# Attention with top-k and a gated FFN on one core: sums over V in units of the last 64 queries over a full 128-row last chunk of keys

## The chip, the cores and the metric

The kernel runs on one core of a Trainium2 chip. The metric is the device time of one execution in microseconds; the time before is the median of three runs. The core's engines work side by side and meet at semaphores: PE (TensorE, matmuls and transposes), DVE (VectorE), ACT (ScalarE), POOL (GpSimd) and SP, which here only issues DMA transfers.

## What is computed

Eight batches, eight heads, 576 queries and keys a head, head dimension 64; everything is fp32. A head's scores are masked to the 32 largest of each query, run through a softmax and multiplied with V. The result is the input of a gated FFN.

```python
def _attn_ref(q, k, v):                      # each (8, 8, 576, 64)
    scores = scale * np.matmul(q, k.transpose(0, 1, 3, 2))
    kth = np.partition(scores, -top_k, axis=-1)[..., -top_k:-top_k + 1]
    scores = np.where(scores >= kth, scores, -1000000000.0)
    scores = scores - np.max(scores, axis=-1, keepdims=True)
    attn = np.exp(scores)
    attn = attn / (np.sum(attn, axis=-1, keepdims=True) + 1e-09)
    return np.matmul(attn, v).astype(np.float32)

def _moe_ref(x, w_gate, w_val, w_out):       # x (4608, 512), d_ff 1536
    g = x @ w_gate
    silu = g * (1.0 / (1.0 + np.exp(-g)))
    return (silu * (x @ w_val) @ w_out).astype(np.float32)
```

## The kernel before

The 576 queries of a head are four groups of 128 and one of 64 (`P` = 128, `J` = 4, `R` = 64, `S` = 576, `JP` = 512). The keys are cut in the same way: four chunks of 128 and a tail of 64. A unit of work is one query group of one pair of heads: `units` lists for each batch the groups `qt` = 0 to 4 and for each group the four pairs of heads, 160 units in all. In an ordinary unit the two heads lie side by side in the free dimension, 2 x 576 scores for each of 128 queries. In a unit of the last 64 queries (`qt == J`, called `last` in the code; 32 units) the two heads are stacked on the partitions: 64 queries of one head on partitions 0 to 63, 64 of the other on 64 to 127, with one row of 576 scores each.

The main loop runs over the units, one step each, with the stages of several units in one step. `scores` (L314, L300 for last units) multiplies Q and K on PE, ACT scales the result into `sc` (L319, L305); `select` finds the 32 largest on DVE (L334, L338); `weigh` runs the exponentials on ACT (L361, L366); `normalize` divides by the sum, on ACT (L384) or POOL (L386). Two steps after a unit's selection `turn` transposes its weights `e` on PE (L400), so that keys come onto the partitions: four chunks of 128 columns into one PSUM bank, then the tail; ACT copies them to `et` (L401). In a last unit the tail is 64 columns, and its transposed form has 64 rows.

`values` (L434), for two units at a time, multiplies V and `et`, with V as the stationary operand. A head's sum is accumulated over its five chunks of keys; the two heads of a pair write to partitions 0 to 63 and 64 to 127 of `av`, and their matmuls alternate. In an ordinary unit the 64-key tail is joined over two heads: `vlast` is a 128x128 block of which the off-diagonal quarters are zero. In a last unit the tail is summed with `v_last`, 64 rows of V for each of the two heads, after the four full chunks: eight matmuls with 128 rows and 64 columns of V and 64 moving columns, then two with 64 rows. ACT copies `av` to `xT` (L450), the input of the FFN.

Blocks of FFN matmuls (`feed`, L578 and L644) are spread between these stages by credits. The order of instructions on PE, DVE, ACT and POOL is the order in which the program writes them, tied at the end of the kernel (L912 on). Within a step PE gets: the scores of a later unit, `values` of two earlier units (in every second step), the scores of one more unit, then pieces of the FFN, the transposes and the pieces that remain.

V of a pair of heads is loaded by `load_v` on SP's queue: the 512 full keys (L243), the tail for last units (L247) and the tail for ordinary units (L250, two transfers). The loads for the next batch are issued right after `values` has read the buffers of this batch for the last time; `slabs` has four buffers for `v` and for `v_last`. POOL's first work is the identity; its next is the rounding of the FFN weights (L121, L122).

Of the kernel before, what the change touches and what calls it, by code (L numbers as in the profile page):

```python
# [10 lines left out]
FP32 = mybir.dt.float32  # L11
# [4 lines left out]
P = 128  # L16
# [9 lines left out]
def kernel(  # L26
# [37 lines left out]
    nc = tc.nc  # L64
    B, H, S, D = q.shape
    DM, DFF = w_gate.shape
    J = S // P
    JP = J * P
    R = S - JP
# [10 lines left out]
    consts = ctx.enter_context(tc.tile_pool(name="consts", bufs=1))  # L80
    ld = ctx.enter_context(tc.tile_pool(name="ld", bufs=2))
    slabs = ctx.enter_context(tc.tile_pool(name="slabs", bufs=4))
# [7 lines left out]
    ident = consts.tile([P, P], FP32, name="ident")  # L90
    make_identity(nc, ident[:])
    NV = 4
    vlast = []
    for i in range(NV):
        vt = consts.tile([P, P], FP32, name=f"vlast{i}")
        nc.vector.memset(vt[:], 0.0)
        vlast.append(vt)
    wg = consts.tile([P, KC, DFF], FP32, name="wg")
    wv = consts.tile([P, KC, DFF], FP32, name="wv")
    wo = consts.tile([P, MC, DM], FP32, name="wo")  # L100
# [136 lines left out]
    def load_v(i):  # L237
        b, hp = pairs[i]
        h = slice(2 * hp, 2 * hp + 2)
        vt = slabs.tile([P, 2, J, D], FP32, tag="v", name="v")  # L240
        v_last = slabs.tile([R, 2, D], FP32, tag="vl", name="v_last")
        vl = vlast[i % NV]
        nc.sync.dma_start(  # L243
            vt[:].rearrange("p h j d -> p h (j d)"),
            v[b, h, 0:JP].rearrange("h (p j) d -> p h (j d)", j=J),
        )
        nc.sync.dma_start(v_last[:], v[b, h, JP:S].rearrange("h p d -> p h d"))  # L247
        for hh in range(2):
            o = hh * R
            nc.sync.dma_start(vl[o : o + R, o : o + R], v[b, 2 * hp + hh, JP:S])  # L250
        vs[i] = (vt, v_last, vl)
# [138 lines left out]
    def turn(n):  # L390

        last = units[n][1] == J
        e = state[n].pop("e")
        et = work.tile([P, 2 * J + 1, P], FP32, tag="et", name="et")
        for c0, cn in ((0, J), (J, 1)) if last else ((0, J), (J, 1), (J + 1, J)):
            ps = ps_t.tile([P, 512], FP32, tag="t", name="etps")
            kl = R if last and c0 == J else P
            for c in range(cn):
                k0 = (c0 + c) * P
                nc.tensor.transpose(ps[0:kl, c * P : (c + 1) * P], e[:, k0 : k0 + kl], ident[:])  # L400
            nc.scalar.copy(  # L401
                et[0:kl, c0 : c0 + cn, :],
                ps[0:kl, 0 : cn * P].rearrange("p (c j) -> p c j", c=cn),
            )
            if c0 == J:
                yield
        state[n]["et"] = et
# [3 lines left out]
    def values(ns):  # L411

        b, qt, hp0 = units[ns[0]]
        last = qt == J
        ql = R if last else P
        av = ps_t.tile([P, 2, P], FP32, tag="t", name="av")
        for i, n in enumerate(ns):
            assert units[n] == (b, qt, hp0 + i)
            vt, v_last, vl = vs[b * NHP + hp0 + i]
            et = state.pop(n)["et"]  # L420
            for c in (*range(J), J) if last else (J, *range(J)):
                kl = R if last and c == J else P
                for hh in range(2):
                    d = slice(hh * R, (hh + 1) * R)
                    if c == J:
                        weights_, at = (v_last[:, hh, :], d) if last else (vl[:, d], None)
                    else:
                        weights_, at = vt[:, hh, c, :], d if last else None
                    moving = (
                        et[0:kl, c, at]  # L430
                        if last
                        else et[:, c + (0 if c == J else hh * (J + 1)), :]
                    )
                    nc.tensor.matmul(  # L434
                        av[d, i, 0:ql],
                        weights_,
                        moving,
                        start=c == (0 if last else J),
                        stop=c == (J if last else J - 1),
                    )  # L440
        c0 = b * S + qt * P
        at = c0
        hps = slice(hp0, hp0 + len(ns))
        while at < c0 + ql:
            kb = at // BLK
            n_c = min((kb + 1) * BLK, c0 + ql) - at
            if kb not in xT:
                xT[kb] = ffn.tile([P, NHP, BLK], FP32, tag="xT", name="xT", bufs=3)
                done[kb] = 0
            nc.scalar.copy(  # L450
                xT[kb][:, hps, at - kb * BLK : at - kb * BLK + n_c],
                av[:, 0 : len(ns), at - c0 : at - c0 + n_c],
            )
            done[kb] += n_c * len(ns)
            at += n_c
# [364 lines left out]
    def finish_units(ns):  # L820
        values(ns)
        for n in ns:
            b, qt, hp = units[n]
            if qt == J and b + 1 < B:
                load_v((b + 1) * NHP + hp)
# [17 lines left out]
    for n in range(NU + 3):  # L843
# [41 lines left out]
        if n < NHP:  # L885
            load_v(n)
# [4 lines left out]
        if 0 <= n - TURN < NU:  # L891
            run(turn(n - TURN))
# [63 lines left out]
```

## Time and profile before

| | |
|---|---|
| runs | 1759.61, 1762.16, 1762.41 us; median 1762.16 |
| profiled execution | 1759.77 us, of which the span from the first to the last instruction is 1758.0 |
| mean granted TensorE clock | 0.974 of full speed |
| tail transposes and others, L400 | 1312 matmul records, 182.9 us busy |
| sums over V, L434 | 2560 records with `v`, 512 with `vlast`, 128 with `v_last` |
| copies of `et`, L401 | 448, 183.4 us busy |
| loads of `v_last` | 32 of 32 KB, 3.1 us from issue to landing |

A record of a matmul says its form as rows x columns of the stationary operand (128*64: 128 rows of contraction, 64 columns) and then the moving operand. Matmuls are pipelined, and the profile models their ends; their starts are taken from the hardware, so the distance from one start to the next tells what each costs a busy PE. The granted clock is the share of full speed that PE had; it is recorded in stretches that are multiples of 3.4 us, at 1.0 or at 0.5.

### The profile page before, as it was taken

How to read it: one execution, taken by the hardware profiler on the slowest of the kernel's cores; microseconds unless marked ns; L12 is line 12 of the kernel's file. 1: busy time of each engine (PE TensorE's matmuls, PEld its weight loads, DVE VectorE, ACT ScalarE, POOL GpSimd, SP SyncE). 2: the span in 40 equal slices, each digit the busy share in tenths (PEclk: the TensorE clock that was granted, in tenths of full speed). 3: DMA queues.
4: the chain of work that ended last, by engine and by line, in shares of the span. 5: the costliest groups of instructions: out<-in, count | busy, mean ns of one | idle time of the engine just before them, and what ended most of it. 6: DMA issues, size and time to landing. Idle time of an engine off the chain costs nothing.

```text
span 1758.0 us, 31754 instructions
## 1 busy us (share of the span) xinstructions
PE 1679.6 (96%) x11408; PEld 1404.5 (80%) x11408; DVE 1476.5 (84%) x3311; ACT 1262.3 (72%) x2901; POOL 798.8 (45%) x910
## 2 busy tenths in 40 slices
PE   5578999999999999999999999999999999999999
PEld 3468588787888788887888878887888878788887
DVE  6999899989889899898899898898988988898300
ACT  7899787777767686768776777777776777676431
POOL 4898534343353425352535334443444433535434
PEclk6698999999999999999999999999999999999999
DMA  7442120003000120002100020000300020000000
GB/s 200 138 120 86 29 68 1 13 2 83 15 13 1 28 70 1 13 12 59 28 13 1 14 70 27 1 13 19 78 2 13 1 57 15 13 1 13 1 13 12
DMA packets 109309, 59.72 MB, mean 34 GB/s; under 512 B 88544, under 2 KB 96992, under 8 KB 109152
## 3 DMA queue, kind: packets, MB, share of 16 engines
q1 hardware_dynamic: 108016, 57.37, 12.5%
q8 instruction: 90, 1.47, 0.4%
q14 instruction: 67, 0.55, 0.1%
q10 hardware_dynamic: 1136, 0.33, 0.1%
HBM read 48.23 MB, written 9.44 MB: 33 GB/s over the span
## 4 chain that ended last, share of the span: by engine, by line
PE 81%; DVE 8%; ACT 8%; POOL 1%; issue 1%; DMA 1%; SPq 0%; ACTq 0%; POOLq 0%
PE f L578 37%; PE av L434 9%; PE x_ps L644 9%; PE s L314 7%; PE y_ps L644 7%; PE etps L400 6%; DVE m L334 4%; DVE e L338 3%; PE f L494 3%; ACT e L366 2%; PE s L300 2%; PE kqps L267 1%; ACT e L361 1%; ACT et L401 1%; PE o_ps L546 1%
## 5 line engine op out<-in xcount | busy, mean ns | idle before, releaser
L334 DVE MAX8 m<-e 128x8 f32<-128x576 f32 x864 | 615.0, 748 | 3.1
L338 DVE MATCH_REPLACE8 e<-m,e 128x576 f32<-128x576 f32 x576 | 423.9, 743 | 0.0
L578 PE MATMUL f<-xT,wg 128*128 128x256 f32 x1536 | 355.0, 381 | 0.0
L578 PE MATMUL f<-xT,wv 128*128 128x256 f32 x1536 | 353.9, 380 | 0.0
L578 PEld LDWEIGHTS f<-xT,wg 128*128 128x128 f32 x1536 | 287.7, 190 | 45.7 <-issue 8.4
L578 PEld LDWEIGHTS f<-xT,wv 128*128 128x128 f32 x1536 | 286.8, 190 | 42.7 <-issue 5.5
L614 POOL TENSOR_TENSOR h<-h,half_g 128x512 f32<-128x512 f32 x96 | 122.5, 1276 | 352.7 <-ACT h L613 336.8
L366 ACT ACTIVATE e<-e,bias 128x576 f32<-128x576 f32 x288 | 221.2, 776 | 34.1 <-POOL bias L349 30.9
L400 PE MATMUL etps<-ident,e 128*128 128x128 f32 (+1 forms) x1312 | 182.9, 281 | 46.7 <-POOL e L386 19.3
L400 PEld LDWEIGHTS etps<-ident,e 128*128 128x128 f32 (+1 forms) x1312 | 154.3, 143 | 76.9 <-POOL e L386 25.3
L338 DVE MATCH_REPLACE8 e<-m,sc 128x576 f32<-128x576 f32 x288 | 211.9, 742 | 0.0
L361 ACT ACTIVATE e<-sc,m 128x576 f32<-128x576 f32 x288 | 211.3, 786 | 0.0
L334 DVE MAX8 m<-sc 128x8 f32<-128x576 f32 x288 | 203.3, 743 | 7.5 <-ACT sc L319 7.5
L319 ACT ACTIVATE sc<-s 128x288 f32<-128x288 f32 x512 | 167.5, 414 | 53.4 <-PE s L314 53.0
L619 POOL TENSOR_TENSOR h<-h,val 128x512 f32<-128x512 f32 x96 | 122.5, 1276 | 178.5 <-ACT val L618 166.0
L386 POOL TENSOR_TENSOR e<-e,tot 128x576 f32<-128x576 f32 x140 | 160.8, 1152 | 87.4 <-DVE tot L380 76.2
L401 ACT COPY et<-etps 128x512 f32<-128x512 f32 (+1 forms) x448 | 183.4, 489 | 12.2 <-PE etps L400 11.7
L314 PE MATMUL s<-kqT 64*128 64x288 f32 x1024 | 171.3, 444 | 16.4 <-ACT et L401 8.3
L379 DVE TENSOR_SCALAR tot<-tot 128x1 f32<-128x1 f32 x228 | 29.4, 146 | 172.0 <-ACT e L366 171.9
L434 PE MATMUL av<-et,v 128*64 128x128 f32 (+1 forms) x2560 | 158.7, 267 | 0.0
L384 ACT ACTIVATE e<-e,tot 128x576 f32<-128x576 f32 x148 | 118.5, 801 | 46.5 <-DVE tot L380 46.2
L314 PEld LDWEIGHTS s<-kqT 64*128 64x128 f32 x1024 | 95.1, 191 | 62.2 <-issue 24.0
(85 smaller groups left out, 2279.0 us busy)
## 6 DMA issues: line engine op xcount, KB each, us to landing
v<-in_v_dram SPq DMA_DIRECT2D x32, 256.0 KB, 3.4
kq_in<-in_k_dram SPq DMA_DIRECT2D x63, 128.0 KB, 2.9
kq_in<-in_q_dram SPq DMA_DIRECT2D x63, 128.0 KB, 3.3
w<-in_moe_w_gate_dram SPq DMA_DIRECT2D x12, 512.0 KB, 3.9
w<-in_moe_w_val_dram SPq DMA_DIRECT2D x12, 512.0 KB, 3.7
w<-in_moe_w_out_dram SPq DMA_DIRECT2D x12, 512.0 KB, 3.6
out_dram<-o SPq DMA_DIRECT2D x38, 128.0 KB, 2.4
out_dram<-o SPq DMA_DIRECT2D x16, 256.0 KB, 2.4
```

The lines of the kernel that those rows point to most:

```text
L314: nc.tensor.matmul(ps[:, 0:half], slab[d, q0 : q0 + P], slab[d, k0 : k0 + half])
L319: nc.scalar.mul(sc[:, i * half : (i + 1) * half], ps[:, 0:half], scale)
L334: nc.vector.max(m[:, t, 8 * r : 8 * r + 8], cur[:, hs])
L338: nc.vector.match_replace(e[:, hs], m[:, t, 8 * r : 8 * r + 8], cur[:, hs], LOWEST)
L361: nc.scalar.activation(e[:, hs], sc[:, hs], AF.Prelu, bias=m[:, t, TOP_K - 1 : TOP_K], scale=-1.0, alpha=SMALL,)
L366: nc.scalar.activation(e[:, hs], e[:, hs], AF.Exp, bias=bias[:, t : t + 1], scale=-1.0 / SMALL, accum_out=tot[:, t : t + 1],)
L386: nc.gpsimd.tensor_tensor(e[:, hs], e[:, hs], tot[:, t : t + 1].to_broadcast([P, S]), ALU.mult)
L400: nc.tensor.transpose(ps[0:kl, c * P : (c + 1) * P], e[:, k0 : k0 + kl], ident[:])
L401: nc.scalar.copy(et[0:kl, c0 : c0 + cn, :], ps[0:kl, 0 : cn * P].rearrange("p (c j) -> p c j", c=cn),)
L434: nc.tensor.matmul(av[d, i, 0:ql], weights_, moving, start=c == (0 if last else J), stop=c == (J if last else J - 1),)
L578: nc.tensor.matmul(ps[:, i, :], w[:, kc, m * P : (m + 1) * P], x[:, kc, :], start=(kc == 0), stop=(kc == KC - 1),)
L644: nc.tensor.matmul(ps, lhsT, T[i][m], start=m == 0, stop=m == MQ - 1)
```

## The change

The tail of a last unit becomes the last 128 keys (448 to 575) in place of the last 64 (512 to 575). Its transpose takes 128 columns of `e`, the copy to `et` 128 partitions, and the two matmuls 128 rows. The keys 448 to 511 thus come in twice, once with the fourth chunk and once here; the second time they meet rows of zeros. V's tail now lies on partitions 64 to 127 of `vtail`, and partitions 0 to 63 are zeroed once, at the start, by four memsets on POOL. The four `vtail` tiles are fixed buffers, taken in turn by the pair's number; the pool's tag `vl` with its four buffers goes. Ordinary units are as they were.

```diff
@@ -90,11 +90,14 @@
     ident = consts.tile([P, P], FP32, name="ident")
     make_identity(nc, ident[:])
     NV = 4
-    vlast = []
+    vlast, vtail = [], []
     for i in range(NV):
         vt = consts.tile([P, P], FP32, name=f"vlast{i}")
         nc.vector.memset(vt[:], 0.0)
         vlast.append(vt)
+        vt = consts.tile([P, 2, D], FP32, name=f"vtail{i}")
+        nc.gpsimd.memset(vt[0 : P - R], 0.0)
+        vtail.append(vt)
     wg = consts.tile([P, KC, DFF], FP32, name="wg")
     wv = consts.tile([P, KC, DFF], FP32, name="wv")
     wo = consts.tile([P, MC, DM], FP32, name="wo")
@@ -238,13 +241,13 @@
         b, hp = pairs[i]
         h = slice(2 * hp, 2 * hp + 2)
         vt = slabs.tile([P, 2, J, D], FP32, tag="v", name="v")
-        v_last = slabs.tile([R, 2, D], FP32, tag="vl", name="v_last")
+        v_last = vtail[i % NV]
         vl = vlast[i % NV]
         nc.sync.dma_start(
             vt[:].rearrange("p h j d -> p h (j d)"),
             v[b, h, 0:JP].rearrange("h (p j) d -> p h (j d)", j=J),
         )
-        nc.sync.dma_start(v_last[:], v[b, h, JP:S].rearrange("h p d -> p h d"))
+        nc.sync.dma_start(v_last[P - R : P], v[b, h, JP:S].rearrange("h p d -> p h d"))
         for hh in range(2):
             o = hh * R
             nc.sync.dma_start(vl[o : o + R, o : o + R], v[b, 2 * hp + hh, JP:S])
@@ -394,13 +397,12 @@
         et = work.tile([P, 2 * J + 1, P], FP32, tag="et", name="et")
         for c0, cn in ((0, J), (J, 1)) if last else ((0, J), (J, 1), (J + 1, J)):
             ps = ps_t.tile([P, 512], FP32, tag="t", name="etps")
-            kl = R if last and c0 == J else P
             for c in range(cn):
-                k0 = (c0 + c) * P
-                nc.tensor.transpose(ps[0:kl, c * P : (c + 1) * P], e[:, k0 : k0 + kl], ident[:])
+                k0 = S - P if last and c0 == J else (c0 + c) * P
+                nc.tensor.transpose(ps[:, c * P : (c + 1) * P], e[:, k0 : k0 + P], ident[:])
             nc.scalar.copy(
-                et[0:kl, c0 : c0 + cn, :],
-                ps[0:kl, 0 : cn * P].rearrange("p (c j) -> p c j", c=cn),
+                et[:, c0 : c0 + cn, :],
+                ps[:, 0 : cn * P].rearrange("p (c j) -> p c j", c=cn),
             )
             if c0 == J:
                 yield
@@ -419,7 +421,6 @@
             vt, v_last, vl = vs[b * NHP + hp0 + i]
             et = state.pop(n)["et"]
             for c in (*range(J), J) if last else (J, *range(J)):
-                kl = R if last and c == J else P
                 for hh in range(2):
                     d = slice(hh * R, (hh + 1) * R)
                     if c == J:
@@ -427,7 +428,7 @@
                     else:
                         weights_, at = vt[:, hh, c, :], d if last else None
                     moving = (
-                        et[0:kl, c, at]
+                        et[:, c, at]
                         if last
                         else et[:, c + (0 if c == J else hh * (J + 1)), :]
                     )
```

## The prediction

> **What bounds the kernel now.** I read the page's busy shares first, then its chain of waits, then busy times by stretch, and last the matmuls around the sums over V in order of time.
>
> ```profile
> PE 1679.6 (96%) x11408; PEld 1404.5 (80%) x11408; DVE 1476.5 (84%) x3311; ACT 1262.3 (72%) x2901; POOL 798.8 (45%) x910
> ...
> PE 81%; DVE 8%; ACT 8%; POOL 1%; issue 1%; DMA 1%; SPq 0%; ACTq 0%; POOLq 0%
> ```
>
> PE is busy 96% of the span and makes 81% of the chain that ended last. A busy PE isn't PE at its peak, so the stretches come next (columns: length, then busy time of PE, weight loads, DVE, ACT, POOL, granted clock, DMA share).
>
> ```profile
> 345.00:600.00 255.00, 252.88 (x1725) 211.79 (x1725) 228.19 (x519) 186.09 (x426) 110.89 (x133) 1.00 0.08 20
> 600.00:900.00 300.00, 297.21 (x2036) 249.57 (x2036) 268.19 (x614) 223.82 (x523) 120.41 (x145) 1.00 0.13 33
> 900.00:1200.00 300.00, 298.78 (x1993) 251.37 (x1992) 269.01 (x615) 221.04 (x508) 127.07 (x150) 1.00 0.07 19
> 1200.00:1500.00 300.00, 296.79 (x2039) 248.19 (x2038) 266.00 (x607) 222.02 (x517) 122.21 (x148) 1.00 0.11 27
> ```
>
> From 345 us on PE stands still for about 1% of the time, at full clock, and DVE has some 11% to spare. What is taken from PE there should come off the end. Now the sums over V. A matmul of fp32 leaves two records (64 matmuls with `v_last` on 64x64 give 128), which I call passes. First a block of a pair of units with the last 64 queries, then one of ordinary units:
>
> ```profile
> 226.64 0.69 PE L434 MATMUL av<-et,v 128*64 128x64 f32 x16
> 227.25 0.33 PE L434 MATMUL av<-et,v_last 64*64 64x64 f32 x4
> 227.52 0.69 PE L434 MATMUL av<-et,v 128*64 128x64 f32 x16
> 228.13 0.33 PE L434 MATMUL av<-et,v_last 64*64 64x64 f32 x4
> 228.39 1.00 PE L314 MATMUL s<-kqT 64*128 64x288 f32 x6
> ...
> 269.63 0.44 PE L434 MATMUL av<-et,vlast 128*64 128x128 f32 x4
> 269.90 1.04 PE L434 MATMUL av<-et,v 128*64 128x128 f32 x16
> 270.77 0.39 PE L434 MATMUL av<-et,vlast 128*64 128x128 f32 x4
> 270.99 1.04 PE L434 MATMUL av<-et,v 128*64 128x128 f32 x16
> ```
>
> No idle is noted in the first block, yet the rate differs. Sixteen passes of form 128*64 go from 226.64 to 227.25, 38 ns each; the four of form 64*64 take 227.25 to 227.52, 68 ns each. In the ordinary block, all of one form, four passes of twice as many columns cost 0.22 us (270.77 to 270.99), 55 ns each. So the tail is dear although it streams least. The starts of single matmuls show where the time lies. Between passes of one form with 64 columns the steps alternate, 7 ns and 52 ns (a pair of heads every 58.5 ns). From the last `v` pass to the first `v_last` pass the step is 152 ns (median of 28 after 340 us), from the last `v_last` pass to the next unit's `v` 148, to the scores that follow 148, and inside the four tail passes 7, 100, 7. A change of tile at the same form costs no such step: `vlast` to `v`, both 128*64 with 128 columns, is 103 ns (104 times), the usual step there, while `v` to the scores' 64*128 is 203. A change of form thus costs about 100 ns, whichever way I compare (152 less 52, 203 less 103).
>
> **The change, part by part.** *Tail matmuls (L434).* They keep their number and order; the form goes from 64*64 to 128*64, that of the `v` passes. For the first unit of a block, last `v` pass to the next unit's first `v` pass is now 152 + 113 + 148 = 413 ns. In one form it is three pair pitches less one short step, 3 x 58.5 - 7 = 169 ns, so 244 ns go. For the second unit the change of form ahead of the scores stays: 413 becomes 52 + 65 + 149 = 266, so 147 go. Together 0.39 us for a block. There are 32 units of this kind in 16 blocks. Fifteen run at full clock: 15 x 0.39 = 5.9 us. The last, at 1690.4 to 1693.3 us, runs at half clock (steps 244, 168, 242, pair pitch 108): 654 becomes 324 - 7 = 317, and 654 becomes about 101 + 115 + 242 = 458, which saves 0.53 us. Sum 6.4 us. Bounds: by changes of form alone, three fewer a block at 100 ns, 16 x 0.3 = 4.8 us; by the whole surplus 6.4. I take 6.4, since the restart inside the tail (100 for 52) follows a change of form each time and nowhere else.
>
> The Trainium skill, "TensorEngine Tiling (Array Packing)", Key Properties, says that changing the tiling mode, not just the tile, drains TensorE; the rows above agree, with 100 ns as the price. A rule of the same page, Theoretical Speedup, speaks against the change: with 64 rows of contraction two row tiles can work at once, up to twice as fast, and 128 rows give that up. If the tail used that today, its two pairs at 58.5 ns would be half price and the change would give back 32 x 58.5 = 1.9 us; by that the sum would be 4.5 us. Here both heads' tails lie on partitions 0 to 63, hence in one row tile, and start 7 ns apart exactly as the 128*64 passes do, so I take nothing off.
>
> *Tail transposes (L400).* Each of 32 takes 128 columns of `e` as weights for 64. Where they run unheld, the step to and from the narrow one is 109 ns, the same as between full ones; no form cost shows. Cost 0; bounds 0 and, if the weight load (108 ns at the least, 140 in the median) were exposed, 32 x 0.03 = 1.0 us.
>
> *Tail copies (L401).* ACT copies 128x128 in place of 64x128. Single copies of 64 partitions took 265 ns in the median (32), of 128 partitions 286 (125). The nearest bounds are 0 and 32 x 0.02 = 0.7 us of ACT. ACT is busy 72%; the copy is made one to two steps ahead of its reader, which hides it. Without that cover it costs the 0.7. I take 0.
>
> *Four memsets on POOL.* They stand right after the identity on POOL's queue. A 128x128 memset there took 0.20 us, so at most 0.8 us, from 1.3 to 2.1 us; POOL then has nothing until 14.27, 12.96 us later, when a weight piece lands. PE's first wait is for the identity, ahead of them. Cost 0; uncovered 0.8.
>
> *Loads.* SP's queue holds the same transfers in the same order with the same waits: 32 loads of 32 KB, now to partitions 64 to 127, into four fixed buffers for a pool of four, released by the same matmuls. Issue was 0.62 us, landing 3.1. Cost 0: they are issued nearly a whole batch ahead of use (from 21.5 us for a use at 227). The zeroed rows are written once and never again, so nothing new waits on POOL.
>
> **How much arrives at the end.** The only PE stalls after 345 us lie once or twice a batch, for instance:
>
> ```profile
> 405.07 2.36 PE av L434 x40
> 407.43 0.02 issue
> 407.45 0.43 ACT xT L450 x2
> 407.88 0.68 ACT e L361
> ...
> 409.80 0.30 ACT sc L319
> 410.11 0.04 issue
> 410.15 0.30 PE etps L400
> ```
>
> PE waits 0.99 us there for ACT, but that ACT work itself began when PE's `av` was done. If PE gets there earlier, ACT does too; the stall moves and does not grow. Two blocks (227 and 248 us) lie ahead of a stretch where DVE makes the chain (316.7 to 346 us); DVE idled 0.90 us for ACT at its start, just more than the 0.78 that could arrive. I count 0.6 of these 0.78 and all else: 6.2 us. On the profiled execution, 1759.77 us (span 1758.0 and 1.8 around it), that gives 1753.6. It was among the faster of the four executions, 2.4 below the median of three, 1762.16; against that median the forecast is **1756.0**.
>
> **Rivals.** *Absorbed (chance 0.15).* A stall takes back what PE gains. For it: nearly every batch has a first tail transpose that waits 0.64 to 0.99 us on ACT, and stalls on POOL's scaling at 1522.58 (2.13 us) begin with chains that pass through POOL. Against: all these chains go back to a PE matmul within the same step. If half is lost: 1762.2 - 3.1 = 1759.1, too little to be told from none.
>
> *It doesn't do what it says (0.05).* The extra 100 ns belong to the tail's buffer or its weights' arrival, not to the form. Then 1762. The unbroken 103 ns from `vlast` to `v` speaks against it.
>
> *Slower by the clock (0.04).* The granted clock went to half for 6.8 us at 319.8 and at 1688.5 us, beside PE stalls of 2.23 and 2.61 us; the stall of 2.13 at 1522.58 did not bring it. If the shifted schedule lengthens the stalls of the saturated stretch past about 2.2 us, each costs 6.8 x 0.5 = 3.4 us. Two would eat the gain; from three on it is slower, 1762.2 - 6.2 + 10.2 = 1766.2. Now one stall there is near that size, the rest under 1 us.
>
> **Numbers.** The forecast has 0.76 and holds 1753 to 1758.5. Its lower edge: the full 6.4 and one half-clock window fewer at the end, 3.4 us, would be 1752.4; its upper edge: 4.8 and the 1.0 of the transposes uncovered, 1758.4. With the absorbed case the range is 1752.6 to 1760. Under 0.2% (3.5 us) this kernel's time can't be told from no change, so faster means below 1758.6: 0.78, the forecast's 0.76 and 0.02 of the absorbed case, where less than half is lost. Within 0.2%: 0.17, the rest of that case and most of the second rival. Slower: 0.05.
>
> **What will show it.** In the changed profile the sums of the last 64 queries have one form, 128*64, for `v` and tail; a block goes from its first pass to the scores in about 1.36 us instead of 1.75 (226.64 to 228.39); the one step of about 150 ns left is that to the scores. Transposes' and `xT` copies' counts are unchanged, and PE's idle in the stretches stays near 1%. I am wrong if the step from `v` to the tail stays at 152 ns, if PE idle grows by what its busy time loses, or if half-clock windows appear between 350 and 1680 us.

## The result and the profile after

The changed kernel took 1753.35 us in the median of six runs (1752.52 to 1754.29), the kernel before 1759.48 in six runs beside it (1758.82 to 1762.41). The ratio is 0.9961, with a 95% interval from 0.9948 to 0.9974: 6.9 us less by the ratio, 6.1 by the medians. The forecast was 6.2 us less and 1756.0 us, worked from a median of three that later runs showed to be 2.7 us high; from the profiled execution the same sum had given 1753.6.

The page of the changed kernel, part 1 and the head of part 4:

```profile
span 1750.7 us, 31758 instructions
...
PE 1673.1 (96%) x11408; PEld 1401.1 (80%) x11408; DVE 1475.4 (84%) x3311; ACT 1262.1 (72%) x2901; POOL 799.2 (46%) x914
...
PE 79%; DVE 10%; ACT 6%; POOL 2%; issue 1%; SPq 1%; DMA 0%; POOLq 0%; ACTq 0%; DVEq 0%
```

PE does the same 11408 matmul records in 6.5 us less of busy time (1679.6 before), and the span is 7.3 us shorter; not all of these 7.3 us are the change's, as the leads below show. POOL has four instructions more, the memsets. The block of a pair of last units that stood at 646 us before now reads, in order of time on PE:

```profile
643.12 0.69 PE L435 MATMUL av<-et,v 128*64 128x64 f32 x16
643.63 0.29 PE L435 MATMUL av<-et,vtail 128*64 128x64 f32 x4
643.75 0.64 PE L435 MATMUL av<-et,v 128*64 128x64 f32 x16
644.22 0.29 PE L435 MATMUL av<-et,vtail 128*64 128x64 f32 x4
644.43 1.24 PE L317 MATMUL s<-kqT 64*128 64x288 f32 x8
```

The tail is now 128*64 like the passes around it. Four tail passes take 643.63 to 643.75, 0.12 us instead of 0.27, and a block goes from 643.12 to 644.43 in 1.31 us; before it was 1.75. By the starts of single matmuls, all blocks at full clock take 1.315 us (1.316 at the most) against 1.753 to 1.755. Step by step, v to tail is 52 ns (152 before), inside the tail 7, 52, 7 (7, 100, 7), tail to v 52 (148), and the one step that stays long is that to the scores, 152.

The records of the weight loads show what the long step is made of. The tail's weight loads (PEld) and passes of one block, before and after:

```profile
646.89 0.20 PEld L434 LDWEIGHTS av<-et,v_last 64*64 64x64 f32 x4
646.90 0.33 PE L434 MATMUL av<-et,v_last 64*64 64x64 f32 x4
```

```profile
643.58 0.20 PEld L435 LDWEIGHTS av<-et,vtail 128*64 128x64 f32 x4
643.63 0.29 PE L435 MATMUL av<-et,vtail 128*64 128x64 f32 x4
```

In one form the load starts 56 ns ahead of its first pass, while the `v` passes still run. Before, it started 150 ns after the start of the last `v` pass, together with its own first pass: none of it was hidden.

PE's standing still did not change. Stretches of the changed kernel (columns as in the prediction):

```profile
345.00:600.00 255.00, 252.82 (x1728) 212.72 (x1725) 227.05 (x519) 187.70 (x432) 110.19 (x134) 1.00 0.08 20
600.00:900.00 300.00, 297.22 (x2045) 250.19 (x2044) 271.59 (x618) 225.44 (x527) 122.26 (x147) 1.00 0.13 33
900.00:1200.00 300.00, 298.76 (x1996) 251.74 (x1995) 269.65 (x619) 220.38 (x505) 127.79 (x152) 1.00 0.07 19
```

PE's busy share in each is that of before to 0.1 us, and PE gets through more records in each. No idle took the place of the time removed in these stretches.

Since PE runs the same instructions in the same order, the n-th matmul of one trace can be set against the n-th of the other. Up to 1485 us the lead of the changed kernel grows in steps, at the blocks only, with small losses between them: at 257 us of the kernel before it is 1.97, at 371 still 1.97, at 550 2.76, at 773 3.60, at 918 4.45, at 1066 5.15, at 1369 5.96, at 1485 6.84. Of the first 1.97, 1.1 to 1.2 were there at 90 us, before any tail had run. That part is scatter of the start and not the change's: a second profile of the changed kernel (below) was 1.65 us behind at 104 us. From 1515 to 1530 us the lead falls by 1.70, for a stretch at half clock that this execution alone of the two had there; from 1680 to 1720 it grows by 2.10: the last two blocks give 1.0 of it (0.44 and 0.59, below), and the changed kernel had one stretch at half clock less there (3.4 us for 6.8).

### The profile page after: what moved, and what is told of

Its sections match the earlier page's. It is cut to its first block, busy times and chain, and to the rows that moved or that the text cites. A ratio compares the mean times of both kernels' runs of the same rounds, so it can differ in the third digit from the quotient of the medians.

```text
span 1750.7 us, 31758 instructions
## 1 busy us (share of the span) xinstructions
PE 1673.1 (96%) x11408; PEld 1401.1 (80%) x11408; DVE 1475.4 (84%) x3311; ACT 1262.1 (72%) x2901; POOL 799.2 (46%) x914
## 4 chain that ended last, share of the span: by engine, by line
PE 79%; DVE 10%; ACT 6%; POOL 2%; issue 1%; SPq 1%; DMA 0%; POOLq 0%; ACTq 0%; DVEq 0%
PE f L579 36%; PE x_ps L645 9%; PE av L435 9%; PE s L317 7%; PE y_ps L645 6%; PE etps L402 6%; DVE m L337 5%; DVE e L341 4%; PE f L495 3%; ACT e L369 2%; PE s L303 2%; PE kqps L270 1%; DVE size L123 1%; PE o_ps L547 1%; ACT e L364 1%
## 5 line engine op out<-in xcount | busy, mean ns | idle before, releaser
L402 PE MATMUL etps<-ident,e 128*128 128x128 f32 x1312 | 183.3, 282 | 47.8 <-POOL e L389 20.8
L402 PEld LDWEIGHTS etps<-ident,e 128*128 128x128 f32 x1312 | 155.1, 144 | 78.3 <-POOL e L389 26.5
```

Of the source, the lines that this page charges most:

```text
L402: nc.tensor.transpose(ps[:, c * P : (c + 1) * P], e[:, k0 : k0 + P], ident[:])
```

## The experiments

The theory: PE pays for a change of form between matmuls, about 100 ns at the step, and 48 ns more at the first long step after it, where 100 stands for 52. The main rivals: the price belongs to the tail's buffer or weights; or the gain came from another of the edits. In the first four, the kernel before took 1759.93 us in the median of 23 runs.

**The form alone put back.** From the changed kernel:

```diff
+                        rows = slice(P - R, P) if last else slice(0, P)
-                        weights_, at = (v_last[:, hh, :], d) if last else (vl[:, d], None)
+                        weights_, at = (v_last[rows, hh, :], d) if last else (vl[:, d], None)
...
-                        et[:, c, at]
+                        et[rows, c, at]
```

> The changed kernel with only the tail matmuls put back to 64 rows: they read partitions 64 to 127 of et and vtail (form 64*64), while the wide transposes, the wide copies, the memsets and the fixed buffers stay. If the change of form is the price: the steps from v to the tail and from the tail on are again about 150 ns, a block takes 1.75 us again, and the whole 6.4 us come back, so the time lies within 1.5 us of the kernel before. If the gain came from another of the edits (buffers, transposes, copies, the start): the time stays 5 to 7 us below the kernel before.

Measured: 1761.49 us in the median, ratio 1.0009 (1.0000 to 1.0017), 1.6 us over the kernel before, a hair outside the 1.5 expected. PE in order of time:

```profile
851.37 0.69 PE L437 MATMUL av<-et,v 128*64 128x64 f32 x16
851.98 0.33 PE L437 MATMUL av<-et,vtail 64*64 64x64 f32 x4
852.25 0.69 PE L437 MATMUL av<-et,v 128*64 128x64 f32 x16
852.86 0.33 PE L437 MATMUL av<-et,vtail 64*64 64x64 f32 x4
853.12 0.51 PE L317 MATMUL s<-kqT 64*128 64x288 f32 x2
```

The block is 1.75 us again, with steps of 152, 148, 152 and 148 ns, although the tail's buffer is `vtail` and everything else is as changed. So all of the gain is in the form. The wide transposes, wide copies, memsets and fixed buffers gave nothing; in the trace they cost 0.10 us over twelve blocks, and by the ratio no more than 0.17%.

**Two narrow tails side by side.** From the kernel before:

```diff
-            for c in (*range(J), J) if last else (J, *range(J)):
+            order = (*range(J), J) if last and i == 0 else (J, *range(J))
+            for c in order:
...
-                        start=c == (0 if last else J),
-                        stop=c == (J if last else J - 1),
+                        start=c == order[0],
+                        stop=c == order[-1],
```

> The kernel before with 64-row tails, but the second unit of a block starts with its tail, so that the two tails stand next to each other: one change of form fewer in a block, the same matmuls in all. If the form is the price: tail to tail is 52 ns, the block takes 1.75 less 0.14 us, and 15 x 0.14 plus some 0.2 at half clock gives 2.3 us less than the kernel before (1.8 to 2.6). If the price belongs to the tail's buffer or its weights: the second tail still begins with a step of about 150 ns and the time does not move.

Measured: 1758.06 us, ratio 0.9989 (0.9980 to 0.9998), that is 1.9 us less. PE:

```profile
846.62 0.69 PE L435 MATMUL av<-et,v 128*64 128x64 f32 x16
847.24 0.45 PE L435 MATMUL av<-et,v_last 64*64 64x64 f32 x8
```

The eight tail passes stand in one group: between the first unit's tail and the second's the step is the ordinary one (51 ns), though the buffer changes there. They take 230 ns from first to last start, and the block 1.608 us, as forecast (1.75 less 0.14). The work is the same, pass for pass; one change of form fewer saved the 0.146 us. That rules out the tail's buffer and weights as the cause, and also the 64 rows by themselves: inside the group the narrow passes keep the ordinary pace.

**Only the second unit narrow.** As the first experiment, with `last and i == 1` for `last`.

> The changed kernel with 64-row tails in the second unit of each block only (the first keeps its 128 rows). If the form is the price: 0.147 us of each block come back, 15 x 0.147 + 0.2 = 2.4, so the time is 4.0 us below the kernel before (3.2 to 4.8), between the two kernels; the step after the second tail stays 150 ns, as in both. If each narrow tail costs the same wherever it stands: half, 3.2 us below.

Measured: 1754.88 us, ratio 0.9974 (0.9962 to 0.9985), 4.6 us less; the sum had said 4.0. PE:

```profile
846.05 0.69 PE L437 MATMUL av<-et,v 128*64 128x64 f32 x16
846.56 0.29 PE L437 MATMUL av<-et,vtail 128*64 128x64 f32 x4
846.68 0.64 PE L437 MATMUL av<-et,v 128*64 128x64 f32 x16
847.25 0.33 PE L437 MATMUL av<-et,vtail 64*64 64x64 f32 x4
847.51 0.76 PE L317 MATMUL s<-kqT 64*128 64x288 f32 x4
```

A block takes 1.460 us: 0.294 less than before, not 0.244. The missing 0.05 us is the restart of the second unit's `v` passes. Their first long step is 100 ns after a narrow tail and 52 after a wide one, and my sum had counted such a restart only inside the tail. The step after the narrow tail is 149, as in both kernels.

**The changed kernel again.** No edit.

> The changed kernel unaltered, beside the others on this chip: 6.4 us below the kernel before by the sum (5.5 to 7.2). If the 1.2 us by which its first profile was ahead at 90 us, before any tail had run, belong to the change, they are there again, and absent where the tails' buffers are those of the kernel before (adjacent tails); if they are scatter of the start they differ from run to run.

Measured: 1753.57 us, ratio 0.9961 (0.9949 to 0.9974). At 104 us this profile was 1.65 us behind the kernel before, the first one 1.20 ahead, and the one with adjacent tails, whose buffers are the old ones, 1.39 ahead: the early difference is scatter.

**Two row tiles.** From the changed kernel, as the first experiment, with `rows = d` for the tail: the second head's tail on partitions 64 to 127, the first head's on 0 to 63.

> The changed kernel with 64-row tails of which the first head's lie on partitions 0 to 63 and the second head's on 64 to 127, two row tiles at once; the first head's tail then multiplies keys 448 to 511 with rows of zeros, so its last 64 keys are left out of the sum. If only the change of form counts: the step into the tail and out of it are 150 ns as with 64 rows on one row tile, a block takes 1.75 us, the time is that of the kernel before within 1.5 us. If two row tiles work faster than one: the steps inside the four tail passes shrink below 7, 100, 7 and the block is shorter than 1.70 us.

Measured: 1759.73 us, ratio 1.0000 (0.9991 to 1.0009), beside 1760.54 for the kernel before. PE:

```profile
848.82 0.69 PE L437 MATMUL av<-et,v 128*64 128x64 f32 x16
849.44 0.33 PE L437 MATMUL av<-et,vtail 64*64 64x64 f32 x4
849.70 0.69 PE L437 MATMUL av<-et,v 128*64 128x64 f32 x16
850.31 0.33 PE L437 MATMUL av<-et,vtail 64*64 64x64 f32 x4
850.57 1.00 PE L317 MATMUL s<-kqT 64*128 64x288 f32 x6
```

The block is 1.753 us, the tail's steps are 7, 100, 6, the same as on one row tile. Two row tiles brought nothing here. The two heads' passes start 7 ns apart in either placement, and only two passes stand side by side; more of them were not tried.

**The tail in the middle.** From the first experiment:

```diff
-            for c in (*range(J), J) if last else (J, *range(J)):
+            order = (0, 1, J, 2, 3) if last else (J, *range(J))
+            for c in order:
```

> The changed kernel with 64-row tails (partitions 64 to 127) that stand after the second of the four full chunks in both units of a block, so that each unit leaves the form and comes back: one change of form more than in the kernel before. If every departure into the other form costs 0.292 us when v follows (100 into the tail, 48 more inside it, 96 out of it, 48 more at the restart of v) and 0.147 when the scores follow, a block takes 1.315 + 2 x 0.292 = 1.90 us against 1.754, and the time is 15 x 0.146 + 0.2 = 2.4 us above the kernel before (1.6 to 3.0). If the price is by the number of narrow tails only: the time of the kernel before.

Measured: 1764.33 us, ratio 1.0020 (1.0011 to 1.0030), 3.5 us more. PE:

```profile
850.18 0.45 PE L438 MATMUL av<-et,v 128*64 128x64 f32 x8
850.56 0.33 PE L438 MATMUL av<-et,vtail 64*64 64x64 f32 x4
850.82 0.69 PE L438 MATMUL av<-et,v 128*64 128x64 f32 x16
851.43 0.33 PE L438 MATMUL av<-et,vtail 64*64 64x64 f32 x4
851.70 0.45 PE L438 MATMUL av<-et,v 128*64 128x64 f32 x8
852.08 0.76 PE L317 MATMUL s<-kqT 64*128 64x288 f32 x4
```

The passes are those of the first experiment, but the block is 1.902 us (1.90 forecast): it enters the narrow form twice and leaves it for `v` twice. The time came out 0.5 us above the expected range, and its own interval (1.9 to 5.3 us more) overlaps it. One 3.4 us stretch at half clock fell into this profile; the next two runs ask why.

All of them side by side. The third column is the change of a block times sixteen; the fourth is what the kernel gains (minus) or loses (plus) on the kernel before between 257 and 1485 us, where twelve blocks lie, from the n-th matmul of both traces. The last column has intervals of 1.5 to 2.3 us to either side.

| kernel | block, us | 16 blocks, us | 12 blocks, in the trace | by the ratio, us |
|---|---|---|---|---|
| changed | 1.315 | -7.0 | -4.87, again -4.85 | -6.9 |
| second unit narrow | 1.460 | -4.7 | -3.26 | -4.6 |
| tails side by side | 1.608 | -2.3 | -1.74 | -1.9 |
| before | 1.754 | 0 | 0.00 (a second profile) | 0 |
| form put back | 1.754 | 0 | +0.10 | +1.6 |
| two row tiles | 1.753 | 0 | +0.23 | 0.0 |
| tail in the middle | 1.902 | +2.4 | +2.01 | +3.5 |

Counted from the first `v` pass to the scores that follow, these blocks have one, two, three, four, four, four and five changes of form. Each change adds 0.145 to 0.148 us to the block, and the times follow within their intervals.

One difference in form shows no price. The narrow transposes of the kernel before (128*64 between others of 128*128) stand at the usual 109 ns on both sides, as the prediction noted. Every other change of form in its trace after 340 us that PE meets at full clock and without a wait costs 93 to 100 ns at the step, also where the columns alone differ: from the 64*64 tail to the scores' 64*128 the step is 148 for 52. Why the transposes are spared is open.

**The clock at the long stall.** The kernel before and the changed kernel, each once more, without an edit.

> The kernel before once more, for the granted clock at PE's stall of 2.1 us near 1520 us. If the clock falls when a stall lies wholly inside one of the 3.41 us stretches in which it is set: half clock for 3.4 us after it when it begins in the first 0.37 of a stretch, full clock when it begins later. If the change of the kernel brings it: full clock whatever the place.

> The changed kernel once more, for the same: half clock for 3.4 us near 1515 us when the stall begins in the first 0.37 of a stretch of 3.41 us, full clock when later. If the change of the kernel brings it: half clock whatever the place.

Measured: the stall near 1520 us began at 0.83 of a stretch in the kernel before and at 0.94 in the changed one, and the clock stayed full in both (1758.41 and 1751.11 us, one execution each). The second says that the change does not bring the half clock: the first two profiles of the changed kernel had it, this one didn't. The first alone fits both. Both stalls began late in a stretch, so the half of the forecast that says half clock was not put to the test by these two.

## Why the prediction was right, point by point

*What bounds the kernel* held: PE's time in the middle of a saturated stretch came off the end. Of the 12 x 0.439 = 5.27 us that the blocks between 257 and 1485 us lost, 4.87 arrived, 92%.

*Tail matmuls, 0.39 us a block:* the mechanism was right and the size too small, by 0.05 us. The long step into the tail, the restart inside it and the step out of it went as forecast. The sum stopped at the start of the next unit's first `v` pass. After that pair too a step of 100 ns stood for 52, in the trace that the prediction was made from. With this restart a block saves 0.439, and sixteen of them save 15 x 0.439 + 0.59 = 7.2 us in place of 6.4; the last block, at half clock, went from 2.92 to 2.33 us.

*Tail transposes, copies, memsets, loads, 0 each:* nearly. With all of them in and the old block length, twelve blocks lost 0.10 us (form put back) and 0.23 us (two row tiles). The kernel with the tails side by side, which has the old transposes, copies and buffers, lost nothing: 1.74 us arrived of 12 x 0.146 = 1.75. Which of these edits costs the tenths was not taken apart. The memsets show where they hide, between the identity and the first weight piece on POOL:

```profile
1.02 0.29 POOL masks.py:199 TENSOR_SCALAR_AFFINE_SELECT ident<-ident 128x128 f32<-128x128 f32 x1
1.26 0.63 POOL L99 MEMSET vtail<- 64x128 f32 x4
14.13 1.29 POOL L124 TENSOR_TENSOR size<-size,w 128x512 int32<-128x512 int32 x1 [12.24 <-DMA w<-in_moe_w_val_dram]
```

*The discount for the first batch, 0.2 us:* the step was in the wrong place. The first two blocks, ahead of the DVE chain, arrived whole (1.09 to 1.97, 0.88 us). Small losses came later, the largest, 0.16 us, in the scores that follow the block at 1031 us of the kernel before. ACT's copies of earlier scores to `sc` and PE's scores after the block, before and after:

```profile
1031.83 1.34 ACT L319 ACTIVATE sc<-s 128x288 f32<-128x288 f32 x4
1033.01 1.24 PE L314 MATMUL s<-kqT 64*128 64x288 f32 x8
```

```profile
1027.38 1.34 ACT L322 ACTIVATE sc<-s 128x288 f32<-128x288 f32 x4
1028.12 1.40 PE L317 MATMUL s<-kqT 64*128 64x288 f32 x8
```

ACT makes these copies in 1.34 us, from 0.57 us after the block's first pass, in both kernels. Before, PE came to its scores 1.75 us after that pass, when the copies were nearly done. Now it comes after 1.31 us, its weight loads are released one by one as copies end (1028.13, 1028.43, 1028.73), and the scores take 1.40 us instead of 1.24. It is the same in all three profiles of the changed kernel; with only the second unit narrow, where the block is 0.145 us longer, this place loses nothing. So ACT took this part back. That is read from the traces; no run changed ACT's work. It is what the rival called absorbed speaks of, in another place than the transposes it named.

*Rivals.* Absorbed: 8% was, over the twelve blocks, not half. It doesn't do what it says: refuted by the tails side by side. The clock: a half-clock stretch did appear in the saturated part, at 1516 us, and cost 1.7 us, but not by the step that I gave. The stall had not grown (2.13 before, 2.14 after), so the threshold of about 2.2 us was wrong; see below. Half clock between 350 and 1680 us was also one of the prediction's own signs of being wrong; two of three profiles of the changed kernel show it, and the third shows that the change does not bring it whatever the place. The rule of row tiles working at once (the Trainium skill, "TensorEngine Tiling (Array Packing)", Theoretical Speedup) was weighed and set aside; the run with two row tiles shows no gain from it for these tails, 7, 100, 6 ns on two tiles and 7, 100, 7 on one.

The gain worked out 7.2 us for the forecast's 6.4, and about 0.4 of it was lost on the way for the 0.2 allowed; what remains, 6.8, stands well with the 6.9 of the ratio. That the forecast's 6.2 came so near is in part luck: the blocks gave 0.8 us more than the sum and the losses took 0.2 us more, and the ratio's interval (4.6 to 9.2 us) could not tell 6.2 from 6.8; the blocks in the traces do. The 1753.35 us lie only 0.35 above the lower end of the forecast's range, 1753, because its base was the high median of three.

## What to carry to other kernels

A matmul that is smaller than its neighbours can cost more than one padded to their form: here a change of form cost PE about 100 ns at the step and 48 at the next, beside the 58 ns in which a pair of passes gets through when nothing changes. The same price stands in this kernel wherever FFN matmuls and scores meet (309 for 216 ns going in, 332 for 236 coming out), which this change left as it is. Look for it in the starts of neighbouring matmuls, since the profile counts it as busy; and where a form must change, put the odd ones side by side. Count the restart on both sides of the odd group, too.

## What the runs showed of the hardware beside that

The stall of 2.13 to 2.15 us near 1520 us is in all ten profiles of this study. The granted clock is recorded in multiples of a stretch of 3.413 us, whose bounds can be laid out from its recorded changes. In four profiles the stall began at 0.09, 0.16, 0.21 and 0.37 of a stretch, so that it ended inside it: all four had half clock for the next 3.4 us. In six it began at 0.72 to 0.94 and ran over the bound: none had. The stall's length doesn't decide it: of three that took 2.144 us, two had half clock and one had not. Stretches of the changed kernel, first and third profile (clock is the third column from the end):

```profile
1516.50:1519.90 3.40, 3.40 (x10) 2.69 (x9) 2.47 (x8) 3.08 (x9) 1.83 (x2) 0.50 0.00 0
```

```profile
1517.50:1520.90 3.40, 3.40 (x19) 3.06 (x20) 2.38 (x8) 3.28 (x9) 1.41 (x3) 1.00 0.00 0
```

The same work right after the same stall gets through 10 matmul records in 3.4 us in the one and 19 in the other. A stall of 63% of a stretch was enough in these four, where one stretch held all of it. The Trainium skill, "TensorE: Matmul & The Clock Gate", Part 1, says that the activity window runs freely and does not start with the kernel, which fits that the place of the stall in it differs from one execution to the next. It is worth 1.7 us of scatter here, a quarter of the effect measured. For longer stalls the place does not explain all. The one of 2.23 us near 318 us brought half clock in all ten profiles, though in seven it ran over a bound. Of those of 2.6 us near 1685 us, one that began at 0.47 left the clock full, one at 0.48 brought 6.8 us of half clock. That stays open.
